# Attention values of four heads in one load: 64 value products of 256 columns over four column groups, one collecting product, and the output projection all 512 wide

## The chip, the cores and the metric

The kernel runs on one core of one Trainium2 chip. The metric is the device time of one execution in microseconds (us). The kernel before takes 235.41 us, the median of three runs (235.37 to 235.57). The profile shows one execution of the same program: its span, from the first instruction to the last, is 233.7 us. All times inside the program are counted from the start of that span.

## The reference

One decoding step of a transformer block for two batch rows (`B = 2`), everything in float32. A conditioning vector `c` gives six modulation vectors. The attention has 32 query heads that share 8 key and value heads (four query heads to one), and looks at the last 4096 positions of the cache. After it come the output projection `wo` and a two-layer network with SiLU.

```python
mod = (_silu(c) @ w_mod).reshape(2, 6, 1, -1)         # sa, ca, ga, sb, cb, gb
h = _layernorm(x) * (1 + ca) + sa
q = (h @ wq), split into 32 heads of 128
k = k_cache[:, :, Sk - W:, :]                         # W = 4096, 8 heads, each used by 4 query heads
v = v_cache[:, :, Sk - W:, :]
p = _softmax(q . k * 128 ** -0.5)
o = p . v                                             # 32 heads of 128
x = x + ga * (o @ wo)                                 # wo: 4096 x 512
h = _layernorm(x) * (1 + cb) + sb
x = x + gb * (_silu(h @ w1) @ w2)                     # w1: 512 x 1792, w2: 1792 x 512
```

What is read from HBM is almost all of the work: 32 MiB of keys, 32 MiB of values, 8 MiB of `wq`, 8 MiB of `wo`, 6 MiB of `w_mod`, and 3.5 MiB each of `w1` and `w2`.

## The kernel before

**The ring.** All large loads go through one buffer in SBUF, `slots`, of 8 slots with 4096 floats per partition each (L68). `stream(n)` (L70) hands out the next n slots; for an even n it first moves on to a multiple of n. All these loads are issued on one queue, that of SyncE (SP in the profile), in the order of the code. A load into a slot waits on SP until everything that read the slot's last content is done, and so does every load behind it.

**The stages.** First `w_mod` (3 slots) and `wq` (4 slots) are loaded, and the modulation and the queries are computed. Then come eight steps (`STEPS`, one for each pair of key heads and batch row), and behind them the output projection, the second normalization and the network.

**One step.** `load_pair` (L77) loads the keys of two heads, 4 MiB, 32768 bytes per partition, into two slots, and, one step later, the values of the same two heads in the same way. `keys(s, j)` (L356) transposes a quarter of the keys on VectorE (DVE), 32x32 blocks at a time; there are four buffers for these quarters (L55). `scores(s, j)` (L366) multiplies them on TensorE (PE). `maxima` (L382) and `exponentials` (L400) make the softmax's numerators, and `turn` (L415) brings them into the form in which they are the weights of the value products: `ptb`, 16 blocks of 32 columns, two buffers of it.

**The value products.** `weighted(s)` (L442) multiplies the values of one step: 16 products of 512 columns each. Every product writes 32 partitions of the result; four products that follow one another write four different groups of 32 partitions, which TensorE works on side by side (four column groups). Since the data are float32, the profile counts two matmul instructions for one product. ScalarE (ACT) copies the 128x512 result to SBUF, and `collect(s)` (L460) adds it with four small products into `o_all`, which is kept in PSUM over all eight steps.

**The order.** `inorder` keeps the instructions of one engine in the order of the code. The loop (L475 to L500) runs the scores of step s ahead of the value products of step s-1. The values of the last step are loaded last, and `weighted(7)` and `collect(7)` stand at the end.

**Behind the steps.** `on` (L534) divides `o_all` by the sums of the softmax, and four products with `quad` (`oq`, L537) and a copy turn it into `oTn`, the weights of the output projection. `busy(n)` (L562) issues n products that write to `junk` and are read by nobody; `busy(6)` (L576) stands ahead of the projection. The projection with `wo` (loaded in two pieces, 24 and 8 of its 32 rows per partition) has 28 products of 512 columns over four column groups (`acc_o`, L577) and 16 products of 128 columns that write straight to `ao` (L586). `gather` (L546) adds the four groups of `acc_o` into `ao`: ACT copies the first half to SBUF, DVE the second, and four products follow. Then come, each waiting for the one before, the transposition `aoT`, the mean `mean_b`, `hT_b`, the products with `w1` (`hid`, L627), the SiLU on DVE and ACT, whose result is `uT`, and the products with `w2`: `acc_yw` (8 of 14 rows of `w2`), `acc_y`, another `gather`, and `acc_l`. `w1` is loaded in two pieces and `w2` in four, of which the first (8 rows) is the largest. In the ring `wo` takes the slots 0 to 3, the first piece of `w1` the slots 4 and 5, its second the slot 6, the first piece of `w2` the slot 7, and the other pieces of `w2` the slots 0 to 2.

Of the kernel before, what the change touches and what calls it, by code (L numbers as in the profile page):

```python
# [8 lines left out]
F32 = mybir.dt.float32  # L9
# [14 lines left out]
def adaln_block(  # L24
# [30 lines left out]
    ktp = ctx.enter_context(tc.tile_pool(name="ktp", bufs=4))  # L55
# [47 lines left out]
    for b in range(B):  # L103
# [46 lines left out]
    id16, mix = const([P, 16], "id16"), const([P, 16, 2], "mix")  # L150
# [3 lines left out]
    nc.gpsimd.tensor_mul(  # L154
        mix,
        id16[:, :, None].to_broadcast([P, 16, 2]),
        half[:, None, :].to_broadcast([P, 16, 2]),
    )
    odd = const([P, 2], "odd")
    nc.vector.tensor_reduce(  # L160
        odd, ident.rearrange("p (a r) -> p r a", r=2), axis=AX.X, op=ALU.add
# [13 lines left out]
    selh = const([P, 4, 4 * HQ - 8], "selh")  # L175
    nc.gpsimd.memset(selh, 0.0)
    nc.gpsimd.tensor_copy(
        selh[:, :, 2 * HQ - 8 : 2 * HQ].rearrange("p m (e g) -> p m e g", e=2),
        id4.rearrange("p (e m g) -> p m e g", e=2, g=G),
# [26 lines left out]
    ptb = [const([P, 16, 2, 16], f"ptb{i}") for i in range(2)]  # L206
# [132 lines left out]
    o_all = bank("O", "o_all")[:, :DH]  # L339
# [26 lines left out]
    def scores(s, j):  # L366
# [3 lines left out]
        i, b = divmod(s, B)  # L370
        for c in range(2):
            for e in range(2):
                r, h = 64 * e + 32 * c, 2 * i + e
# [41 lines left out]
    def turn(s):  # L415
# [9 lines left out]
        tp = bank("C", f"pT{s}")[:, : 2 * P]  # L425
        for i in range(4):
            inorder(nc.tensor.matmul(  # L427
                tp[32 * i : 32 * i + 32, :],
                mix.rearrange("p v e -> p (v e)"),
                zp.rearrange("p y t x -> p (y t) x")[:, :, 4 * i : 4 * i + 4],  # L430
                start=True,
                stop=True,
            ))
        for e in range(2):
            inorder(nc.scalar.activation(  # L435
                ptb[s % 2][:, :, e, :],
                tp.rearrange("p (w z) -> p w z", z=16),
                AF.Copy,
                scale=odd[:, e : e + 1],
            ))  # L440
# [291 lines left out]
```

## Time and profile before

| what | us |
|---|---|
| median of three runs | 235.41 (235.37 to 235.57) |
| span of the profiled execution | 233.7 |
| DVE busy | 115.6 (49% of the span) |
| PE busy | 161.1 (69%), in 1070 matmul instructions |
| ACT busy | 28.5 (12%) |
| POOL busy | 10.5 (4%) |
| read from HBM | 97.53 MB, 417 GB/s over the span |
| share of DMA waits in the chain that ended last | 60% |

A row of a timeline gives the start in us from the span's start, the duration in us, the engine, the line of the program, the operation, the result and the operands, and how many instructions are merged in it; in brackets stands how long the engine was idle before, and what ended the wait. PE is matmul, PEld the loading of weights for it. A row of the windows gives a stretch, its length, the busy time of the engines in it with the count of instructions, the TensorE clock that was granted (1.00 is full speed), the mean busy share of the core's 16 DMA engines, and what they moved. Over a short stretch the share can come out a little above 1.

### The profile page before, as it was taken

To read this page: it belongs to the slowest core of one execution; us is meant where nothing else is said; L and a number is where in the kernel's file an instruction comes from. 1 tells how busy PE (TensorE), PEld (TensorE's weight loads), DVE (VectorE), ACT (ScalarE), POOL (GpSimd) and SP (SyncE) were. 2 spreads that over 40 slices of the span, in tenths; PEclk is the share of its full clock that TensorE was granted. 3 is DMA by queue.
4 is the path that set the end of the run, shared out by engine and by line. 5 is a ranking of instruction groups with operands and counts; after the bars stand their busy time and mean duration, and the time that the engine had idled before them with its cause. 6 is when DMAs were issued, how large, how long until landed. Compare 5 with 4: busy or idle time off the path is not lost.

```text
span 233.7 us, 2571 instructions
## 1 busy us (share of the span) xinstructions
PE 161.1 (69%) x1070; PEld 43.3 (19%) x1070; DVE 115.6 (49%) x179; ACT 28.5 (12%) x64; POOL 10.5 (4%) x35
## 2 busy tenths in 40 slices
PE   0004916859577839797598749759759779789684
PEld 0001401201111111211120201202112122324222
DVE  0007240278894758695197089259559540101232
ACT  2000210000311120120210201111020120102020
POOL 2004710000000000000000000000000000000000
PEclk9999985979999977999979999988997997999999
DMA  7998998999999999999999999999999999989991
GB/s 269 446 542 359 404 494 359 446 444 421 415 421 449 446 437 415 426 426 446 449 437 409 418 437 449 449 421 412 426 444 449 443 421 437 463 367 437 424 404 57
DMA packets 3794, 97.68 MB, mean 418 GB/s; under 512 B 432, under 2 KB 456, under 8 KB 968
## 3 DMA queue, kind: packets, MB, share of 16 engines
q1 hardware_dynamic: 3768, 97.53, 97.1%
q8 instruction: 8, 0.13, 0.2%
q14 instruction: 2, 0.02, 0.0%
q10 hardware_dynamic: 16, 0.00, 0.0%
HBM read 97.53 MB, written 0.00 MB: 417 GB/s over the span
## 4 chain that ended last, share of the span: by engine, by line
DMA 60%; issue 18%; DVE 14%; PE 6%; POOL 0%; SPq 0%; POOLq 0%; ACT 0%
DMA slots<-in_A_k_cache_dram 22%; DMA slots<-in_A_wq_dram 15%; DMA slots<-in_A_v_cache_dram 12%; DMA slots<-in_B_w_dram 12%; DVE kT L361 11%; PE o L448 2%; PE q L302 2%; DVE zp L420 1%; PE acc_yw L661 1%; DVE xp L418 1%; PE qr L323 0%; PE acc_y L671 0%; DVE qT L315 0%; POOL qg L319 0%; SPq L109 0%
## 5 line engine op out<-in xcount | busy, mean ns | idle before, releaser
L361 DVE STREAM_TRANSPOSE kT<-slots 128x1024 f32<-128x1024 f32 x64 | 73.7, 1212 | 23.7 <-DMA slots<-in_A_k_cache_dram 23.6
L374 PE MATMUL s<-kT,qbd 128*32 128x512 f32 x256 | 68.6, 693 | 19.1 <-DVE kT L361 18.0
L448 PE MATMUL o<-slots,ptb 128*32 128x512 f32 x256 | 30.8, 624 | 2.1 <-DMA slots<-in_A_v_cache_dram 2.1
L374 PEld LDWEIGHTS s<-kT,qbd 128*32 128x32 f32 x256 | 9.6, 113 | 68.4 <-DVE kT L361 63.4
L269 PE MATMUL m_a<-slots,scT 128*32 128x256 f32 x32 | 4.4, 506 | 20.5 <-DVE scT L261 20.5
L302 PE MATMUL q<-slots,hq_T 128*32 128x512 f32 x64 | 8.3, 680 | 7.0 <-DMA slots<-in_A_wq_dram 7.0
L448 PEld LDWEIGHTS o<-slots,ptb 128*32 128x32 f32 x256 | 8.1, 114 | 17.9 <-issue 17.8
L404 ACT COPY bias<-bp 128x1 f32<-128x1 f32 x8 | 1.3, 159 | 77.0 <-PE bp L402 77.0
L384 DVE TENSOR_REDUCE mx<-s 128x1 f32<-128x512 f32 x8 | 5.5, 691 | 9.6 <-PE s L374 9.6
L565 PE MATMUL junk<-quad,id 128*32 128x512 f32 x22 | 10.2, 595 | 0.0
L420 DVE TENSOR_TENSOR zp<-xp,quarter 128x1024 f32<-128x1024 f32 x8 | 9.8, 1225 | 0.2
L435 ACT ACTIVATE ptb<-pT,odd 128x256 f32<-128x256 f32 x16 | 6.7, 472 | 25.6 <-PE pT L427 25.6
L255 DVE STREAM_TRANSPOSE cT<-xc 128x128 f32<-128x128 f32 x1 | 0.4, 401 | 16.7 <-DMA xc<-in_c_dram 16.7
L427 PE MATMUL pT<-zp,mix 128*32 128x256 f32 x64 | 5.7, 428 | 3.6 <-DVE zp L420 3.5
L458 ACT COPY ob<-o 128x512 f32<-128x512 f32 x8 | 4.7, 585 | 26.1 <-PE o L448 26.1
L272 PE MATMUL m_sp<-slots,scT 128*32 128x512 f32 x32 | 7.4, 738 | 0.0
L386 PE MATMUL mT<-ident,mx 128*1 128x128 f32 x16 | 3.0, 270 | 6.3 <-DVE mx L384 6.3
L315 DVE STREAM_TRANSPOSE qT<-q 128x512 f32<-128x512 f32 x2 | 1.4, 717 | 11.7 <-PE q L302 10.2
L418 DVE STREAM_TRANSPOSE xp<-pr 128x512 f32<-128x512 f32 x8 | 5.5, 686 | 3.4 <-ACT pr L406 3.4
L579 PE MATMUL acc_o<-slots,oTn 128*32 128x512 f32 x56 | 6.2, 593 | 0.7 <-DMA slots<-in_A_wo_dram 0.7
L466 PE MATMUL o_all<-ob,selh 128*64 128x128 f32 x64 | 6.0, 316 | 0.8 <-ACT ob L458 0.8
L550 DVE COPY acc_o_sb<-acc_o 128x256 f32<-128x256 f32 x1 | 0.4, 425 | 12.4 <-ACT acc_o_sb L549 12.4
(140 smaller groups left out, 93.8 us busy)
## 6 DMA issues: line engine op xcount, KB each, us to landing
slots<-in_A_k_cache_dram SPq DMA_DIRECT2D x8, 4096.0 KB, 27.4
slots<-in_A_v_cache_dram SPq DMA_DIRECT2D x8, 4096.0 KB, 27.6
slots<-in_w_mod_dram SPq DMA_DIRECT2D x1, 6144.0 KB, 17.1
slots<-in_A_wo_dram SPq DMA_DIRECT2D x1, 6144.0 KB
slots<-in_B_w_dram SPq DMA_DIRECT2D x1, 2688.0 KB
slots<-in_A_wo_dram SPq DMA_DIRECT2D x1, 2048.0 KB, 29.5
slots<-in_B_w_dram SPq DMA_DIRECT2D x1, 2048.0 KB
slots<-in_B_w_dram SPq DMA_DIRECT2D x1, 896.0 KB
```

What stands on the lines that cost most here:

```text
L272: nc.tensor.matmul(m_sp[r, :], scT[:, k, :], cd[:, g], start=(k == 0), stop=(k == 3))
L302: nc.tensor.matmul(q_ps[n][32 * g : 32 * g + 32, :], hq_T[:, k, :], wv[:, n, g], start=(k == 0), stop=(k == 3),)
L361: inorder(nc.vector.transpose(kT[s, j][:, 32 * c : 32 * c + 32, :], kt[s].rearrange("p (n j r) -> p j n r", j=4, r=32)[:, j, 32 * c : 32 * ...
L374: inorder(nc.tensor.matmul(s_ps[s][r : r + 32, :], qbd[h // 4][:, h % 4, b, j, :], kT[s, j][:, 32 * c : 32 * c + 32, e:32:2], start=(j == ...
L418: inorder(nc.vector.transpose(xp, pr[s]))
L420: inorder(nc.vector.tensor_mul(zp, xp[:, None, :, 0:16].to_broadcast([P, 4, 16, 16]), quarter[:, :, None, None].to_broadcast([P, 4, 16, 16 ...
L427: inorder(nc.tensor.matmul(tp[32 * i : 32 * i + 32, :], mix.rearrange("p v e -> p (v e)"), zp.rearrange("p y t x -> p (y t) x")[:, :, 4 * ...
L435: inorder(nc.scalar.activation(ptb[s % 2][:, :, e, :], tp.rearrange("p (w z) -> p w z", z=16), AF.Copy, scale=odd[:, e : e + 1],))
L448: inorder(nc.tensor.matmul(o_ps[s][r : r + 32, :], ptb[s % 2][:, w].rearrange("p e z -> p (e z)"), vt[s].rearrange("p (c w m f d) -> p c f ...
L466: inorder(nc.tensor.matmul(o_all[r : r + 64, :], selh[:, m, lo : lo + 2 * HQ], o_sb[s][:, m * DH : (m + 1) * DH], start=(s == 0 and m < 2) ...
L565: inorder(nc.tensor.matmul(junk[0:32, :], id4, quad.rearrange("p m y -> p (m y)"), start=True, stop=True,))
L579: inorder(nc.tensor.matmul(acc[32 * g : 32 * g + 32, :], oTn[:, q, :], wot[q], start=(q < 4), stop=(q >= 24),))
```

## The change

**Loads.** `load_heads` takes the number of heads: keys still come two heads at a time (two slots, 32768 bytes per partition), values four heads at a time (four slots, 65536 bytes per partition, 8 MiB). The steps now run through all heads of one batch row before the other, so that two neighbouring steps share one load of values. Since `wq` ends at slot 7, the keys always fall on slots 0 to 3 and the values always on slots 4 to 7.

**Value products.** `turn` makes 64 blocks of weights for a pair of steps (`ptb`, one buffer, each step fills half of the columns), with eight products of 256 columns in place of four, and two ACT copies of twice the size. `weighted` runs once for two steps: 64 products of 256 columns over four column groups. ACT copies the result in two halves and scales each (`own`). `collect` is one product of 256 columns, and `o_all` has 64 rows of 256, whose two halves DVE adds (`of_all`) ahead of `on`.

**Behind the steps.** The projection has 32 products of 512 columns and no small ones. `gather` copies both halves on ACT, and for the projection issues one `busy` product ahead of its four products.

```diff
-    ktp = ctx.enter_context(tc.tile_pool(name="ktp", bufs=4))
+    ktp = ctx.enter_context(tc.tile_pool(name="ktp", bufs=3))
...
-    def load_pair(cache, s):
-        i, b = divmod(s, B)
-        t = stream(2)
+    def load_heads(cache, b, h, heads):
+        t = stream(heads)
         nc.sync.dma_start(
             t,
-            cache[b, 2 * i : 2 * i + 2, SK - W :, :].rearrange("e (u n) d -> u e (n d)", u=P // 2),
+            cache[b, h : h + heads, SK - W :, :].rearrange("e (u n) d -> u e (n d)", u=P // heads),
         )
         return t
...
+    id16, mix = const([P, 16], "id16"), const([P, 2, 8, 2, 2], "mix")
...
+    quad4 = const([P, 4], "quad4")
+    nc.vector.tensor_reduce(
+        quad4, ident.rearrange("p (a r) -> p r a", r=4), axis=AX.X, op=ALU.add
     )
...
+    selh = const([P, 2 * LO + 16], "selh")
...
+    own = const([P, 2], "own")
+    nc.vector.tensor_reduce(
+        own, id4.rearrange("p (e m g) -> p m e g", e=4, m=2), axis=AX.XY, op=ALU.add
     )
...
-    ptb = [const([P, 16, 2, 16], f"ptb{i}") for i in range(2)]
+    ptb = const([P, 32, 2, 4, 8], "ptb")
...
-    o_all = bank("O", "o_all")[:, :DH]
+    o_all = bank("O", "o_all")[: B * HQ, : 2 * DH]
...
-    def fetch(s):
+    def head(s):
+        b, i = divmod(s, HKV // 2)
+        return b, 2 * i
+    def fetch_keys(s):
         if s < STEPS:
-            kt[s] = load_pair(k_cache, s)
-        if s > 0:
-            vt[s - 1] = load_pair(v_cache, s - 1)
+            kt[s] = load_heads(k_cache, *head(s), 2)
+    def fetch_values(i):
```

The body of `turn` behind `zp`, `weighted` and `collect` after the change:

```python
    def turn(s):
...
        tp = bank("C", f"pT{s}")
        for f in range(2):
            for i in range(4):
                inorder(nc.tensor.matmul(
                    tp[32 * i : 32 * i + 32, 2 * P * f : 2 * P * (f + 1)],
                    mix[:, f].rearrange("p u a e -> p (u a e)"),
                    zp.rearrange("p y t x -> p (y t) x")[:, :, 4 * i : 4 * i + 4],
                    start=True,
                    stop=True,
                ))
        for e in range(2 * (s % 2), 2 * (s % 2) + 2):
            inorder(nc.scalar.activation(
                ptb[:, :, :, e, :].rearrange("p w y z -> p (w y) z"),
                tp.rearrange("p (v z) -> p v z", z=8),
                AF.Copy,
                scale=quad4[:, e : e + 1],
            ))
    def weighted(i):
        o_ps[i] = bank("D", f"o{i}")[:, : 2 * DH]
        runs = vt[i].rearrange(
            "p (h c w y m f d) -> p (h c) f w y m d", h=2, c=2, w=4, y=2, m=2, f=2
        )
        for v in range(64):
            w, r = v // 2, 32 * (v % 4)
            inorder(nc.tensor.matmul(
                o_ps[i][r : r + 32, :],
                ptb[:, w, v % 2].rearrange("p e z -> p (e z)"),
                runs[:, w // 8, w // 4 % 2, w % 4, v % 2],
                start=(v < 4),
                stop=(v >= 60),
            ))
        o_sb[i] = once.tile([P, 2 * DH], F32, tag="wide", name=f"ob{i}")
        for m in range(2):
            c = slice(m * DH, (m + 1) * DH)
            inorder(nc.scalar.activation(
                o_sb[i][:, c], o_ps[i][:, c], AF.Copy, scale=own[:, m : m + 1]
            ))
    def collect(i):
        b, h = head(2 * i)
        lo = LO - (HQ * b + G * h)
        inorder(nc.tensor.matmul(
            o_all, selh[:, lo : lo + 2 * HQ], o_sb[i], start=(i == 0), stop=(2 * i + 2 == STEPS)
        ))
```

The loop, and what stands behind it:

```diff
-    fetch(0)
...
+    fetch_keys(0)
+    fetch_keys(1)
+    fetch_values(0)
     keys(0, 0)
-    for s in range(STEPS + 1):
-        if s < STEPS:
-            fetch(s + 1)
-            scores(s, 0)
-        if s > 0 and s != STEPS - 1:
-            turn(s - 1)
-        if s > 1:
-            collect(s - 2)
-        if s == 2:
+    for s in range(STEPS):
+        scores(s, 0)
+        for j in range(1, 4):
+            keys(s, j)
+            scores(s, j)
+        fetch_keys(s + 2)
+        maxima(s)
+        exponentials(s)
+        if s % 2 == 0:
+            keys(s + 1, 0)
+        turn(s)
+        if s == 1:
             place(1)
-        if s < STEPS:
-            for j in range(1, 4):
-                keys(s, j)
-                scores(s, j)
-            maxima(s)
-            exponentials(s)
-        if s < STEPS - 2:
-            keys(s + 1, 0)
-        if s > 0:
-            weighted(s - 1)
-        if s == STEPS - 2:
-            turn(s)
-            keys(s + 1, 0)
-    collect(STEPS - 1)
+        if s % 2:
+            weighted(s // 2)
+            fetch_values(s // 2 + 1)
+            collect(s // 2)
+            if s + 1 < STEPS:
+                keys(s + 1, 0)
...
-    on = once.tile([P, B, DH], F32, tag="xp", name="on")
+    nc.tensor.matmul(
+        lp[:R, 0:1], rx.rearrange("p b i e g -> p (b i e g)"), ones, start=True, stop=True
+    )
...
+    of_all = once.tile([R, DH], F32, tag="zp", name="of_all")
+    nc.vector.tensor_reduce(
+        of_all, o_all.rearrange("r (m d) -> r d m", m=2), axis=AX.X, op=ALU.add
+    )
+    on = once.tile([R, B, DH], F32, tag="xp", name="on")
     for b in range(B):
-        nc.vector.tensor_scalar(on[:, b, :], o_all, rlb[:, b : b + 1], None, op0=ALU.mult)
+        nc.vector.tensor_scalar(on[:, b, :], of_all, rlb[:, b : b + 1], None, op0=ALU.mult)
...
-    def gather(acc, wide, name, start, stop):
...
+    def gather(acc, wide, name, start, stop, fill=0):

         sb_ = once.tile([P, D], F32, tag="wide", name=name)
-        nc.scalar.copy(sb_[:, : D // 2], wide[:, : D // 2])
-        inorder(nc.vector.tensor_copy(sb_[:, D // 2 :], wide[:, D // 2 :]))
+        for c in (slice(0, D // 2), slice(D // 2, D)):
+            inorder(nc.scalar.copy(sb_[:, c], wide[:, c]))
+        if fill:
+            busy(fill)
...
-    for q in range(28):
...
             start=(q < 4),
-            stop=(q >= 24),
+            stop=(q >= 28),
         ))
-    for q in range(28, 32):
-        for g in range(4):
-            inorder(nc.tensor.matmul(
-                ao[32 * g : 32 * g + 32, :],
-                oTn[:, q, :],
-                wot[q][:, g * P : (g + 1) * P],
-                start=(q == 28),
-                stop=False,
-            ))
-    gather(ao, acc, "acc_o_sb", False, True)
+    gather(ao, acc, "acc_o_sb", True, True, fill=1)
```

Two places show how the instructions move. The first is the queue of SP at the end of the loop: the last loads of keys and values and the first of the weights behind them. Before (the last column is partitions x floats per partition):

```order
L82 DMA slots<-in_A_k_cache_dram 128x1x8192
L82 DMA slots<-in_A_v_cache_dram 128x1x8192 x2
L93 DMA slots<-in_A_wo_dram 128x12288
L93 DMA slots<-in_A_wo_dram 128x4096
L93 DMA slots<-in_B_w_dram 128x5376
```

After:

```order
L81 DMA slots<-in_A_k_cache_dram 128x1x8192 x2
L81 DMA slots<-in_A_v_cache_dram 128x1x16384
L92 DMA slots<-in_A_wo_dram 128x12288
L92 DMA slots<-in_A_wo_dram 128x4096
L92 DMA slots<-in_B_w_dram 128x5376
```

Before, the last two loads ahead of `wo` are values of 4 MiB each; after, it is one load of values of 8 MiB, and both last loads of keys stand ahead of it.

The second place is PE from the last value products to the products with `w1` (`o` are the value products, `acc_o` and `ao` the projection, `hid` the products with `w1`). Before:

```order
L448 MATMUL o_900<-slots,ptb_150 32x512 x16
L466 MATMUL o_all<-ob_917,selh 64x128 x4
L539 MATMUL oq<-on,quad 128x64 x4
L565 MATMUL junk<-quad,id_58 32x512 x6
L579 MATMUL acc_o<-slots,oTn 32x512 x28
L588 MATMUL ao<-slots,oTn 32x128 x16
L552 MATMUL ao<-acc_o_sb,id_58 32x128 x4
L565 MATMUL junk<-quad,id_58 32x512
L614 MATMUL mean_b<-ks,mean_139 128x2
L565 MATMUL junk<-quad,id_58 32x512
L627 MATMUL hid<-slots,hT_b 32x448 x8
```

After:

```order
L464 MATMUL o_976<-slots,ptb 32x256 x64
L482 MATMUL o_all<-ob_1041,selh 64x256
L547 MATMUL oq<-on,quad 128x64 x4
L559 MATMUL junk<-quad,id_58 32x512 x6
L589 MATMUL acc_o<-slots,oTn 32x512 x32
L559 MATMUL junk<-quad,id_58 32x512
L576 MATMUL ao<-acc_o_sb,id_58 32x128 x4
L559 MATMUL junk<-quad,id_58 32x512
L615 MATMUL mean_b<-ks,mean_142 128x2
L559 MATMUL junk<-quad,id_58 32x512
L628 MATMUL hid<-slots,hT_b 32x448 x8
```

The 16 value products of 512 columns at the end have become 64 of 256; the 16 small products of the projection are gone and four wide ones have come; a product that writes `junk` stands between the projection and its gathering.

More of the change, by code (lines that the diff above doesn't have):

```diff
@@ L539, in adaln_block @@
         nc.tensor.matmul(
-            oq, quad[:, j, :], on[:, :, 32 * j : 32 * j + 32], start=(j == 0), stop=(j == 3)
+            oq, quad[:R, j, :], on[:, :, 32 * j : 32 * j + 32], start=(j == 0), stop=(j == 3)
         )
@@ L576, in adaln_block @@
     busy(6)
-    for q in range(28):
+    for q in range(32):
         g = q % 4
```

119 lines of the change are left out of this document (43 added, 76 removed).

## The prediction

> **What bounds the kernel now.** I read the page's slices and the windows first (is there a stretch in which the DMA engines are idle?), then the chain that ended last, then the timeline of the tail, where the change puts its longest new piece.
>
> ```profile
> span 233.7 us, 2571 instructions
> DMA  7998998999999999999999999999999999989991
> 58.00:192.00 134.00, 102.00 (x610) 23.86 (x606) 89.77 (x105) 19.91 (x50) 0.49 (x2) 0.94 1.01 435
> 126.84 27.70 DMA slots<-in_A_k_cache_dram
> 154.54 0.02 issue
> 165.61 27.61 DMA slots<-in_A_v_cache_dram
> 193.21 0.14 issue
> 193.35 5.37 PE o L448 x32
> 198.74 27.57 DMA slots<-in_B_w_dram
> 226.30 0.14 issue
> 226.44 1.92 PE acc_yw L661 x16
> ```
>
> The DMA engines are busy from the first slices to the last but one. In the eight steps (58 to 192 us) their share is 1.01 at 435 GB/s, with PE busy 102 and DVE 90 of 134 us. A load of keys lands at 154.54, the last values at 193.21: four loads of 4 MiB in 38.67 us, 9.67 us each. So the steps are bound by the transfers and compute is hidden. Only what stands behind a last landing counts: the chain leaves the DMA at 193.21 for the value products of the last step, goes back to it, and leaves it at 226.30 for good, when the large piece of `w2` lands. Whether compute or that landing ends last is read from the tail:
>
> ```profile
> 186.21 3.64 PE L448 MATMUL o<-slots,ptb 128*32 128x512 f32 x32
> 188.81 0.13 PEld L448 LDWEIGHTS o<-slots,ptb 128*32 128x32 f32 x4 [0.30 <-issue]
> 189.88 22.84 SPq L93 DMA_DIRECT2D slots<-in_B_w_dram  x6
> 193.35 5.34 PE L448 MATMUL o<-slots,ptb 128*32 128x512 f32 x32 [2.11 <-DMA slots<-in_A_v_cache_dram]
> 198.80 0.58 ACT L458 COPY ob<-o 128x512 f32<-128x512 f32 x1 [7.53 <-PE o L448]
> 199.44 0.66 PE L466 MATMUL o_all<-ob,selh 128*64 128x128 f32 x8 [0.75 <-ACT ob L458]
> 201.91 5.34 PE L565 MATMUL junk<-quad,id 128*32 128x512 f32 x12
> 207.91 6.22 PE L579 MATMUL acc_o<-slots,oTn 128*32 128x512 f32 x56 [0.66 <-DMA slots<-in_A_wo_dram]
> 213.91 1.08 PE L588 MATMUL ao<-slots,oTn 128*32 128x128 f32 x32
> 214.23 0.37 ACT L549 COPY acc_o_sb<-acc_o 128x256 f32<-128x256 f32 x1 [14.85 <-PE acc_o L579]
> 214.71 0.42 DVE L550 COPY acc_o_sb<-acc_o 128x256 f32<-128x256 f32 x1 [12.43 <-ACT acc_o_sb L549]
> 215.65 0.32 DVE L604 STREAM_TRANSPOSE aoT<-ao 128x128 f32<-128x128 f32 x1 [0.52 <-PE ao L552]
> 217.11 1.04 PE L565 MATMUL junk<-quad,id 128*32 128x512 f32 x2
> 217.42 0.17 DVE L618 TENSOR_TENSOR hT_b<-dT,cbT 128x8 f32<-128x8 f32 x1
> 219.46 1.71 PE L627 MATMUL hid<-slots,hT_b 128*32 128x448 f32 x16 [1.30 <-DMA slots<-in_B_w_dram]
> 225.36 0.21 DVE L657 TENSOR_TENSOR uT<-z,sgh 128x28 f32<-128x28 f32 x1
> 226.44 1.92 PE L661 MATMUL acc_yw<-slots,uT 128*32 128x512 f32 x16 [0.76 <-DMA slots<-in_B_w_dram]
> ```
>
> The reader is to see three covers, each a place where PE waited for a transfer although the compute ahead of it was done. The `junk` products stream 12 times 0.43 us (the pace in the PEld row: 0.30 idle and 0.13 loading for each group) from 201.91, so PE was free at 207.07 and waited for `wo` until 207.91: cover 0.84. `hT_b` was ready at 217.59 and the two `junk` passes were through at 217.97, but `hid` waited for `w1` until 219.46: cover 1.49. `uT` was ready at 225.57, some 0.1 later PE could have begun, and `acc_yw` began at 226.44: cover 0.77. In all 3.1 us. A delay of the last value products costs nothing up to that, and its full length beyond.
>
> **The change, part by part.** I add up against the profiled execution; the 1.7 us between its span (233.7) and the median (235.41) lie outside the program and are left as they are.
>
> *Loads.* Bytes are the same, and 435 GB/s over 134 us leave no pauses to remove: 0, so the last values land at 193.21 again. Values now have one buffer of four slots, so `weighted` must be over before the next values can be issued; behind each load of values two of keys are queued, 2 x 9.67 = 19.3 us of transfer, against some 7 to 9 us of products. The first piece of `w1` (issued at 189.88 in the row above) now waits for the last value products, until about 202; ahead of it 8 MiB of `wo`, 19.3 us, run until about 212. That wait holds up all loads behind it on SP, but 10 us of transfers hide it: 0.
>
> *Steps.* Larger copies for `ptb`, eight `pT` products for four, one fewer `kT` buffer: hidden by the transfers, since the busiest engine (PE, 102 of 134 us) has 32 us to spare there: 0.
>
> *Last value products.* They now process 8 MiB, not 4, behind the last landing. What is the price of 64 products of 256 columns, 128 instructions, in groups of four?
>
> ```profile
> 27.56 0.39 PE L269 MATMUL m_a<-slots,scT 128*32 128x256 f32 x3
> 27.78 0.39 PE L269 MATMUL m_a<-slots,scT 128*32 128x256 f32 x3
> 193.30:196.70 3.40, 3.35 (x19) 0.53 1.07 463
> 196.70:198.70 2.00, 1.99 (x20) 0.95 0.91 393
> ```
>
> The `m_a` products are also 256 columns over four column groups; at full clock one group follows the other after 0.22 us, half of the 0.43 of 512 columns. So 32 groups need 6.9 us and 0.2 for the last to end, 7.08 against 3.64 (the row at 186.21, full clock): +3.44. At 193.3 PE had been idle, and ran 3.4 us at clock 0.53, which cost 5.34 - 3.64 = 1.70. PE is idle there again, so the same 1.70 stays in the sum: 8.78 for 5.34. Bounds: no slow stretch at all, -1.7; one of twice the length, +1.7.
>
> *From there to `oTn`.* ACT copies two halves of 128 columns for 0.58 in one piece; `collect` streams 2 x 256 columns, as each half of the array did before (4 x 128): 0 each. New is the sum of the halves on DVE:
>
> ```profile
> L384 DVE TENSOR_REDUCE mx<-s 128x1 f32<-128x512 f32 x8 | 5.5, 691 | 9.6 <-PE s L374 9.6
> L116 DVE TENSOR_REDUCE id<-ident 128x32 f32<-128x128 f32 x1 | 0.4, 368 | 0.0
> ```
>
> 256 elements lie between 368 and 691 ns, about 475; less something for `on`, which then reads half the rows: +0.4 (0.2 to 0.6).
>
> *Projection.* The six `junk` products stay ahead of it in PE's order. The shift so far is 3.84, less the cover of 0.84: it begins 3.0 later, at 210.9, and `wo` has landed by then or lands on the way. Four wide products for sixteen narrow: eight instructions more in two groups, +0.86. The narrow ones (213.91 to 214.99) covered the two copies of `gather`; now the copies stand bare behind the last product, 0.1 less than before since both are ACT's, and the new `junk` product runs beside them. So `aoT` starts at 215.65 + 3.0 + 0.86 - 0.1 = 219.4.
>
> *To the end.* +3.73 there, less the cover of 1.49 at `hid`: +2.24; less 0.77 at `acc_yw`: +1.47. In the last `gather` the second copy is about 0.08 shorter: -0.08. **Sum: +1.4**, a span of 235.1 and a time of **236.8 us** (+0.6%).
>
> **A rule against the change.** The Trainium skill, TensorE: Matmul & The Clock Gate, Part 3 (The mechanism), says that weights load beside a running matmul only when the row group differs; all these products use all rows, so by it four loads would stand bare ahead of each group. The trace disagrees: the PEld row shows 0.13 within a pace of 0.43, which is the streaming alone.
>
> **The rivals.**
>
> *Weight loads are not hidden at 256 columns.* There are 32 groups with loads of 0.13 in a pace of 0.215 that leaves little room. If they stand bare, 32 x 0.13 = +4.2 more, all beyond the covers: 241.0. Against it stand the `m_a` rows. Chance 0.06.
>
> *The values' single buffer opens gaps.* If products, their weights and `place(1)` together outlast the 19.3 us of keys, each of the three later loads of values starts late; at 2 us each, 242.8. The 10 us of room speak against it. Chance 0.04.
>
> *The 65536-byte load lands earlier: not slower.* The load of `wq` has such rows too:
>
> ```profile
> 1.93 35.23 DMA slots<-in_A_wq_dram
> 48.23 2.37 DVE L361 STREAM_TRANSPOSE kT<-slots 128x1024 f32<-128x1024 f32 x2 [1.25 <-DMA slots<-in_A_k_cache_dram]
> ```
>
> It lands at 37.16, and the keys behind it only 11.07 us later, though a load takes 9.67: as if `wq` were 1.4 ahead of the stream. If the last values come 1.4 earlier for that reason, the delay of 1.47 is gone and `acc_yw` waits for `w2` again: 235.4, or 235.3 with the shorter copy. It decides from 1.0 us on. Against it: it is one event, and may be a hold-up of the keys. Chance 0.18 (0.14 of it within 0.2%).
>
> *Fewer loads save a fixed price: faster.* If each load cost 2 us beyond its bytes, four fewer save 8: 227.4. The 435 GB/s leave no room for it. Chance 0.02. The Trainium skill, DMA: Bandwidth & Descriptors, Anatomy of one DMA, fits 2.0 us plus the bytes at 436 GB/s to one DMA; back to back the trace shows 4.19 MB in 9.67 us, the bytes alone.
>
> Something else, around no change: 0.04.
>
> **How the numbers follow.** The forecast holds 0.66, with 235.9 to 238.5 as its own range (the slow stretch shorter or longer by half, the reduction's bounds). The range reaches down to the rival that is not slower: 235.2 to 238.5. What a measurement of this kernel can tell is about 0.2%, 0.47 us. Slower: 0.66 + 0.06 + 0.04 = 0.76. Within: 0.14 and 0.03 of the rest, 0.17. Faster: 0.04 + 0.02 + 0.01 = 0.07.
>
> **What would show it.** The last `o` group should start near 193.3 and take 8.8 us with a first stretch near clock 0.5; `acc_o` should start near 210.9 with no wait for `wo`; `hid` near 221.7 with no wait for `w1`; `acc_yw` should wait for `uT`, near 227.9, not for a DMA. The DMA row should stay at 9 through the steps. An `o` group over 11 us speaks for the weight loads, digits under 9 for the single buffer, a landing near 192 for the earlier load. Any of them makes the prediction wrong.

## The result, and the profile after

The changed kernel takes 241.56 us (median of six runs, 240.73 to 245.92), against 235.44 us (235.30 to 235.66) for the kernel before on the same chip: a ratio of 1.0247, with an interval from 1.0231 to 1.0263. One of the six (245.92 us) is a slow run (over 1.5% above the fastest), as is one run each of x2, x3, x4 and x9 below, the profiled ones of x3 and x9 among them; the ratios use the fast runs alone, and the median of the five fast ones here is 241.41, 6.0 us more than before. The prediction said slower, but by 1.4, and its range ended at 238.5.

The page of the profiled execution (240.73 us) first: the span, the share of the DMA engines in 40 slices, and the shares of the chain that ended last.

```profile
span 238.9 us, 3043 instructions
...
DMA  7998989999998999999999998999999999999930
...
PE 60%; DVE 15%; DMA 15%; ACT 6%; issue 2%; SPq 0%; DVEq 0%; ACTq 0%
```

The transfers still run through the steps as before: the DMA row has its 9 in all slices but a few. Yet the chain, which was 60% DMA, is now 60% PE. Something on the engines ends after the transfers. The timeline from the landing of the keys of step 6 to the last value products, in the changed kernel, shows it:

```profile
164.44 9.13 DVE L373 STREAM_TRANSPOSE kT<-slots 128x1024 f32<-128x1024 f32 x8 [9.52 <-DMA slots<-in_A_k_cache_dram]
174.76 0.69 DVE L396 TENSOR_REDUCE mx<-s 128x1 f32<-128x512 f32 x1 [1.19 <-PE s L386]
...
176.28 2.35 DVE L373 STREAM_TRANSPOSE kT<-slots 128x1024 f32<-128x1024 f32 x2
178.57 0.66 DVE L430 STREAM_TRANSPOSE xp<-pr 128x512 f32<-128x512 f32 x1
179.26 1.23 DVE L432 TENSOR_TENSOR zp<-xp,quarter 128x1024 f32<-128x1024 f32 x1
180.40 6.87 DVE L373 STREAM_TRANSPOSE kT<-slots 128x1024 f32<-128x1024 f32 x6
...
188.47 0.69 DVE L396 TENSOR_REDUCE mx<-s 128x1 f32<-128x512 f32 x1 [1.20 <-PE s L386]
...
191.59 0.71 DVE L430 STREAM_TRANSPOSE xp<-pr 128x512 f32<-128x512 f32 x1 [1.53 <-ACT pr L418]
192.34 1.23 DVE L432 TENSOR_TENSOR zp<-xp,quarter 128x1024 f32<-128x1024 f32 x1
...
193.71 1.94 PE L440 MATMUL pT<-zp,mix 128*32 128x256 f32 x16 [0.94 <-DVE rl L535]
195.70 1.26 ACT L448 ACTIVATE ptb<-pT,quad 128x512 f32<-128x512 f32 x2 [4.14 <-PE pT L440]
197.02 8.45 PE L464 MATMUL o<-slots,ptb 128*32 128x256 f32 x128 [1.38 <-ACT ptb L448]
```

The bracket of the last row decides it: the products wait for ACT's copy into `ptb`, their weights, and not for a DMA as before. They start at 197.02 instead of 193.35, 3.67 later. From the landing of step 6's keys (DVE starts at 164.44, when its wait for the DMA ends) to the weights' end at 196.96 there are 32.5 us of work in sequence: 16 transpositions, two maxima, two exponentials, two turns. Behind that landing only the keys of step 7 and the last values are still to come, three loads' worth, 3 x 9.67 = 29.0 us. So the last values were there at about 193.4 (164.4 + 29.0); the weights came 3.5 us after them.

In the kernel before, the same piece of its timeline was:

```profile
173.93 9.13 DVE L361 STREAM_TRANSPOSE kT<-slots 128x1024 f32<-128x1024 f32 x8 [2.12 <-DMA slots<-in_A_k_cache_dram]
...
189.66 0.61 PE L427 MATMUL pT<-zp,mix 128*32 128x256 f32 x8
190.42 0.84 ACT L435 ACTIVATE ptb<-pT,odd 128x256 f32<-128x256 f32 x2
```

There the last products needed the weights of step 7 alone. From 173.93 to 191.26 these took 17.3 us, against 19.3 us of transfers behind the landing: 2 us to spare. The change joins two steps in each product. Two steps take nearly twice as long on the engines, but only three loads, not four, stand behind the landing that starts them.

The tail of the changed kernel:

```profile
206.91 0.42 DVE L539 TENSOR_REDUCE of_all<-o_all 64x128 f32<-64x256 f32 x1 [13.02 <-PE o_all L482]
208.98 4.91 PE L559 MATMUL junk<-quad,id 128*32 128x512 f32 x11
213.76 7.43 PE L589 MATMUL acc_o<-slots,oTn 128*32 128x512 f32 x61
222.49 0.32 DVE L605 STREAM_TRANSPOSE aoT<-ao 128x128 f32<-128x128 f32 x1 [13.13 <-PE ao L576]
224.50 2.01 PE L628 MATMUL hid<-slots,hT_b 128*32 128x448 f32 x16
230.95 1.92 PE L662 MATMUL acc_yw<-slots,uT 128*32 128x512 f32 x16
235.37 0.63 SPq L705 DMA_DIRECT2D out_dram<-yo  x1
```

In the kernel before, three places in this tail waited for a DMA: the covers of the prediction. None of these waits is left. The table sets each place against the kernel before (the output's DMA was issued at 231.07 there); its last column is the first experiment below.

| place | predicted shift | shift of the change | without step 7's turn (x1) |
|---|---|---|---|
| start of the last `o` | 0 | +3.67 | +0.26 |
| first `junk` | +3.84 | +7.07 | +4.25 |
| `aoT` | +3.73 | +6.84 | +4.01 |
| `hid` | +2.24 | +5.04 | +2.20 |
| `acc_yw` | +1.47 | +4.51 | +1.68 |
| output's DMA issued | +1.4 | +4.30 | +1.47 |
| end of the span | +1.4 | +5.2 | +1.7 |

### The profile page after: what moved, and what is told of

Read it like the earlier page. It is cut to its first block, busy times and chain, and to the rows that moved or that the text cites. A ratio compares the mean times of both kernels' runs of the same rounds, so it can differ in the third digit from the quotient of the medians.

```text
span 238.9 us, 3043 instructions
## 1 busy us (share of the span) xinstructions
PE 154.7 (65%) x1310; PEld 54.7 (23%) x1310; DVE 114.7 (48%) x180; ACT 30.5 (13%) x66; POOL 10.3 (4%) x35
## 4 chain that ended last, share of the span: by engine, by line
PE 60%; DVE 15%; DMA 15%; ACT 6%; issue 2%; SPq 0%; DVEq 0%; ACTq 0%
PE s L386 20%; PE o L464 15%; DMA slots<-in_A_wq_dram 15%; PE pT L440 7%; DVE zp L432 4%; PE q L309 4%; PE junk L559 4%; DVE kT L373 3%; PE acc_o L589 3%; DVE mx L396 2%; DVE xp L430 2%; ACT ptb L448 2%; ACT pr L418 2%; PE hid L628 1%; PE mT L398 1%
## 5 line engine op out<-in xcount | busy, mean ns | idle before, releaser
L386 PE MATMUL s<-kT,qbd 128*32 128x512 f32 x256 | 48.9, 718 | 2.7 <-DVE kT L373 2.4
L464 PE MATMUL o<-slots,ptb 128*32 128x256 f32 x512 | 36.2, 452 | 4.1 <-ACT ptb L448 4.1
L440 PE MATMUL pT<-zp,mix 128*32 128x256 f32 x128 | 15.5, 631 | 26.4 <-DVE zp L432 25.4
L464 PEld LDWEIGHTS o<-slots,ptb 128*32 128x32 f32 x512 | 17.9, 130 | 23.3 <-issue 8.5
L386 PEld LDWEIGHTS s<-kT,qbd 128*32 128x32 f32 x256 | 11.0, 127 | 36.9 <-DVE kT L373 22.8
L448 ACT ACTIVATE ptb<-pT,quad 128x512 f32<-128x512 f32 x16 | 10.1, 683 | 35.2 <-PE pT L440 35.2
L309 PE MATMUL q<-slots,hq_T 128*32 128x512 f32 x64 | 9.7, 776 | 7.3 <-DMA slots<-in_A_wq_dram 7.3
L440 PEld LDWEIGHTS pT<-zp,mix 128*32 128x32 f32 x128 | 5.4, 158 | 30.0 <-issue 30.0
L589 PE MATMUL acc_o<-slots,oTn 128*32 128x512 f32 x64 | 7.9, 594 | 0.0
L474 ACT ACTIVATE ob<-o,own 128x128 f32<-128x128 f32 x8 | 2.5, 364 | 35.4 <-PE o L464 35.4
```

What stands on the lines that cost most here:

```text
L309: nc.tensor.matmul(q_ps[n][32 * g : 32 * g + 32, :], hq_T[:, k, :], wv[:, n, g], start=(k == 0), stop=(k == 3),)
L386: inorder(nc.tensor.matmul(s_ps[s][r : r + 32, :], qbd[h // 4][:, h % 4, b, j, :], kT[s, j][:, 32 * c : 32 * c + 32, e:32:2], start=(j == ...
L440: inorder(nc.tensor.matmul(tp[32 * i : 32 * i + 32, 2 * P * f : 2 * P * (f + 1)], mix[:, f].rearrange("p u a e -> p (u a e)"), zp.rearrang ...
L448: inorder(nc.scalar.activation(ptb[:, :, :, e, :].rearrange("p w y z -> p (w y) z"), tp.rearrange("p (v z) -> p v z", z=8), AF.Copy, scale ...
L464: inorder(nc.tensor.matmul(o_ps[i][r : r + 32, :], ptb[:, w, v % 2].rearrange("p e z -> p (e z)"), runs[:, w // 8, w // 4 % 2, w % 4, v % ...
L589: inorder(nc.tensor.matmul(acc[32 * g : 32 * g + 32, :], oTn[:, q, :], wot[q], start=(q < 4), stop=(q >= 28),))
```

## The experiments

The theory, A: the last products are late because their weights need both steps' chains. The rivals are named in the expectations. Where not said otherwise, a kernel is an edit of the changed one, and each ratio is to the kernel before on the same chip.

**x1: step 7's turn left out.** Its half of the weights stays that of step 5.

```diff
-        turn(s)
+        if s < STEPS - 1:
+            turn(s)
```

> The changed kernel without the weights of the last step (turn of step 7 is left out, so the last value products use old weights in half of their columns). Theory A (the last value products start 3.5 us late because the two steps ahead of them take 32.6 us from the landing of their first keys, while the transfers in between take only 29.1 us): the products start at the landing, near 193.4 us instead of 197.0, and the time falls by 3 to 3.6 us, to about 238. Theory B (the start is not what costs; all of the extra time lies behind it, in 8 MiB of products and the projection): start and time within 1 us of the changed kernel, about 241.

Measured: 237.26 us (236.67 to 237.78), ratio 1.0077 [1.0058, 1.0096]. In its timeline the last products start at the landing again:

```profile
193.61 9.11 PE L464 MATMUL o<-slots,ptb 128*32 128x256 f32 x128 [1.09 <-DMA slots<-in_A_v_cache_dram]
...
228.12 1.92 PE L663 MATMUL acc_yw<-slots,uT 128*32 128x512 f32 x16
...
232.54 0.63 SPq L706 DMA_DIRECT2D out_dram<-yo  x1
```

With the weights' wait gone, 4.1 us of the 6.0 are gone (0.7 of them lie behind the output's issue; see x9 and x10). What is left, 1.85 us over the kernel before, is close to the 1.4 that I had for the whole change, and the table's last column follows my own terms place by place. The work of the turn itself is left out too, but all of it stands ahead of the start of the products.

**x2: the value products of the first three pairs left out.** Only the last pair's stay.

```diff
-            weighted(s // 2)
+            if s == STEPS - 1:
+                weighted(s // 2)
             fetch_values(s // 2 + 1)
-            collect(s // 2)
+            if s == STEPS - 1:
+                collect(s // 2)
```

> The changed kernel with the value products of the first three pairs of steps left out (only the last pair's products and their collection remain). Theory A (each pair starts anew when its first keys land, so late products of one pair do not push the next): the last products still start near 197 us and the time stays within 1 us, 240 to 242. Theory C (a backlog: PE runs through all pairs without a pause, as the chain that ended last reads, and 9 us of products in each pair push everything behind them): the start moves to the landing at 193.4 or to where the keys allow it, and the time falls by 3 us or more, to 238 or less.

Measured: 241.94 us (241.16 to 245.43), ratio 1.0265 [1.0247, 1.0283]: no gain.

```profile
197.04 9.46 PE L464 MATMUL o<-slots,ptb 128*32 128x256 f32 x128 [1.38 <-ACT ptb L448]
```

The start is the same to 0.02 us without 384 earlier instructions of PE, so no delay adds up from pair to pair. The chain of the changed kernel's page runs through the products of all four pairs and gives PE 60%, and would make one believe that it does. Each pair begins anew at the landing of its keys.

**x3: no six `junk` products ahead of the projection.**

```diff
-    busy(6)
```

> The changed kernel without the six products nobody reads that stand ahead of the projection. Before the change they ended 0.84 us before wo landed; after it they stand between oTn (ready at 209.4) and the projection (214.2), though wo has landed. Theory A: the projection starts near 209.5, 4.7 us earlier, and the time falls by about 4.5 us to 237. Rival D (without them the TensorE clock falls and the projection and what follows run at half speed): the projection takes 10 us or more instead of 7.4 and the time falls by 2 us or less.

Measured: 238.23 us (237.55 to 241.28), ratio 1.0109 [1.0092, 1.0126]; 3.3 less than the change, not the 4.5 of theory A, and more than the 2 of rival D.

```profile
210.02 1.78 PE L547 MATMUL oq<-on,quad 64*128 64x64 f32 x8 [1.11 <-DVE on L544]
...
212.16 9.46 PE L588 MATMUL acc_o<-slots,oTn 128*32 128x512 f32 x64 [0.36 <-DVE oTn L550]
```

The projection now begins as soon as `oTn` is there. In the changed kernel `oTn` is ready at 209.36 and the bulk of the projection begins at 213.76, so some 4.4 us stood to be won, and 3.3 were. Where the other 1.1 us went is not shown. The 9.46 us of the projection here, for about 7.9 in the changed kernel, cannot be put down to the missing products: in this execution the four `oq` products ahead of them are slow already (1.78 us for 1.07).

**x4: values in two halves.** Each half has its own load of 32768 bytes per partition and its own 32 products, in the order of loads of the kernel before; the second half's products run in the next pair's first step, the last pair's at the end.

```diff
+        if s % 2 == 0 and s > 0:
+            weighted(i - 1, 1)
+            fetch_values(i, 1)
...
         if s % 2:
-            weighted(s // 2)
-            fetch_values(s // 2 + 1)
-            collect(s // 2)
+            weighted(i, 0)
+            fetch_values(i + 1, 0)
```

> The changed products and projection, but each load of values in two halves of 32768 bytes per partition, the queue in the old order (keys and half values by turns) and the 64 products in two parts of 32, of which the second runs inside the softmax of the next step; only the last 32 stand behind the last landing. Theory A (late start and 8 MiB behind the last landing are the whole loss): the last 32 products start at the landing near 193.3, take 5.3 us, the three covers swallow what the wide projection and the sum of the halves add, and the time is 235 to 236. Theory E (the 256-column products, the wide projection or the gathering cost by themselves): 237 or more.

Measured: 240.02 us (239.34 to 243.86), ratio 1.0195 [1.0174, 1.0215]. A miss: theory A had 235 to 236, and the time lies in the range of E.

```profile
174.50 2.37 DVE L385 STREAM_TRANSPOSE kT<-slots 128x1024 f32<-128x1024 f32 x2 [6.13 <-DMA slots<-in_A_k_cache_dram]
...
195.20 8.83 PE L477 MATMUL o<-slots,ptb 128*32 128x256 f32 x128 [1.38 <-ACT ptb L460]
```

Yet the rows show the wait of theory A: all 64 products still ran together and still waited for `ptb`. A half of the values has 32 of the 64 blocks of weights, but each block has columns of both steps. So the first half cannot go ahead either: step 7's own chain, with step 6's turn in the middle of it, takes 20.7 us from its keys' landing (174.50 to 195.20), and the two halves behind it 19.3.

**x5: halves, and the keys of both steps ahead of the previous pair's second half.** The copies into `ptb` are taken out of `turn` into `weights`, since `ptb` must keep the previous pair's weights until its second half is through.

```diff
         if s % 2 == 0:
             keys(s + 1, 0)
-        turn(s)
...
+            turn(s)
+        else:
+            if i > 0:
+                weighted(i - 1, 1)
+            fetch_values(i, 1)
+            weights(s - 1)
+            turn(s)
+            weights(s)
...
+            weighted(i, 0)
+            fetch_values(i + 1, 0)
```

> The values in halves of 32768 bytes per partition as in x4, but now the keys of both steps of a pair are queued ahead of the second half of the values before (so k6, k7, second half of v2, first half of v3, second half of v3), and step 7's chain runs while 29 us of transfers stand between its keys' landing and the end. Theory A (the last products wait for weights that need both steps' chains): k7 lands near 164.4, all weights are ready near 187, the first 32 products run near 187, and the last 32 start at the landing, near 193.4, and take 4 to 5.3 us; 235.2 to 236.0 in all, since the first half's work is hidden and the transfers' floor is that of the kernel before. Rival E (the order of the queue does not matter; 64 products of 256 columns with weights of four heads cost the time wherever they stand): 239 to 242, as x4. Rival F (the waits for slots that the new order makes open pauses in the stream): last landing after 195, 237 to 239.

Measured: 242.0 us (240.96 to 243.72), ratio 1.0281 [1.0248, 1.0313]. From its timeline (the row of SPq is the issue of the last load of values):

```profile
182.05 3.66 PE L481 MATMUL o<-slots,ptb 128*32 128x256 f32 x64
185.77 0.54 SPq L89 DMA_DIRECT2D slots<-in_A_v_cache_dram  x1
...
190.07 3.66 PE L481 MATMUL o<-slots,ptb 128*32 128x256 f32 x64 [0.81 <-ACT ptb L464]
199.51 5.34 PE L481 MATMUL o<-slots,ptb 128*32 128x256 f32 x64 [5.78 <-DMA slots<-in_A_v_cache_dram]
```

The weights are now in time: the first half's products run at 190.07 and the second half's wait 5.78 us for a DMA, not for `ptb`. But what rival F describes came true, if not its time (237 to 239). The load they wait for goes into the half buffer that the products at 182.05 read. It could be issued only at 185.77, when the load ahead of it was already through, and the stream paused: the page's slice from 180.3 to 186.3 us shows 155 GB/s, its neighbours 431 and 349. The lateness moved from the weights into the transfers. The time lies in the range of E (239 to 242), but the landing alone accounts for it: the last products start 6.16 later than in the kernel before, and the output's DMA is issued 5.97 later (237.04).

**x6: five `junk` products ahead of step 7's turn.**

```diff
         exponentials(s)
+        if s == STEPS - 1:
+            for _ in range(5):
+                inorder(nc.tensor.matmul(
+                    o_bank[64:96, :],
+                    id4,
+                    quad.rearrange("p m y -> p (m y)"),
+                    start=True,
+                    stop=True,
+                ))
```

> After with five products that nobody reads ahead of step 7's turn, while PE waits for step 7's exponentials; they write rows of the bank that nothing else uses. Nothing is left out. Theory A with the clock as a term of its own: the eight pT products of step 7 run at a higher clock (1.94 down to 1.0 to 1.3 us) and the 64 value products without their slow first stretch (8.45 down to 7.1), so the span falls by 1.5 to 2.3 and the time to 239.2 to 240.0. Rival (the clock is not kept by such products, or what they win is lost again by a lower clock in the projection): 241 to 241.7.

Measured: 240.35 us (239.82 to 242.01), ratio 1.0211 [1.0186, 1.0235]. By the ratios (1.0247 for the change) that is about 0.85 us less, and the span is 238.1 for 238.9; 1.5 to 2.3 were expected.

```profile
190.44 4.48 PE L501 MATMUL o_all<-quad,id 128*32 128x512 f32 x10
...
195.06 1.07 PE L441 MATMUL pT<-zp,mix 128*32 128x256 f32 x16
197.51 7.11 PE L465 MATMUL o<-slots,ptb 128*32 128x256 f32 x128 [1.39 <-ACT ptb L449]
```

Both sizes came as expected: `pT` 1.07 for 1.94, the products 7.11 for 8.45, without a slow stretch. But the five products lasted until 194.9 and held `pT` back from 193.71 to 195.06, 1.35 us, so the products ended only 0.85 earlier (204.62 for 205.47). By this pace three of them would have fitted the gap; whether three keep the clock up was not run.

**x7: the kernel before with the wide projection alone.** The 16 narrow products go, `gather` copies both halves on ACT.

```diff
-    for q in range(28):
+    for q in range(32):
...
-    gather(ao, acc, "acc_o_sb", False, True)
+    gather(ao, acc, "acc_o_sb", True, True, fill=1)
```

> The kernel before with one part of the change alone: all 32 products of the output projection 512 wide, and gather with both copies on ACT and one more product that nobody reads. My prediction put +0.86 on the two groups more and -0.1 on the copies, which the wait of hid for w1 (1.49) swallows whole: 235.2 to 235.6. Rival (the added time is not swallowed, because w1's wait was shorter than the row says or the chain to aoT is longer than 0.76): 236.0 to 236.5.

Measured: 235.88 us (235.71 to 236.17), ratio 1.0014 [1.0006, 1.0023].

```profile
208.30 7.07 PE L581 MATMUL acc_o<-slots,oTn 128*32 128x512 f32 x64 [0.72 <-DMA slots<-in_A_wo_dram]
...
219.47 1.71 PE L620 MATMUL hid<-slots,hT_b 128*32 128x448 f32 x16 [0.32 <-DMA slots<-in_B_w_dram]
...
226.53 1.92 PE L654 MATMUL acc_yw<-slots,uT 128*32 128x512 f32 x16 [0.84 <-DMA slots<-in_B_w_dram]
```

The wider projection is swallowed: `hid` starts at 219.47 as it did at 219.46, and still waits for `w1`. The median is 0.26 us above that of the kernel before on the same chip (235.62), and outside the expected 235.2 to 235.6; the span, 233.7, is that of the kernel before, so the profile shows no place for it.

**x8: x5 with the previous pair's second half between the scores.** Eight products at a time, the last eight behind the maxima, and the next half is fetched right behind them.

```diff
             scores(s, j)
+            if s % 2 and i > 0:
+                weighted(i - 1, 1, j - 1)
```

> As x5, but the 32 products of the second half of a pair's values stand between the scores of the next pair's second step, eight at a time, and not behind its bias. In x5 the last load could be issued only at 186.4, when these products were over, and landed at 199.5. Theory A (only a weights' chain or a late issue puts the last products behind the transfers): the products of pair 2 end near 181, the last load is issued there, 4 us ahead of the end of the load before it, and lands at 193.4 to 194.5; the last 32 products start there and take 3.6 to 5.3; 235.3 to 237.0 in all, no slower than before by more than 0.7%. Rival E (64 products of 256 columns cost their time wherever they stand): 239 or more. Rival G (the eight-product pieces hold up the scores and so the weights of pair 3 by 3 us or more): the first half's products run at 193 or later and the last 32 behind them, 237 to 239.

Measured: 239.22 us (238.54 to 239.39), ratio 1.0146 [1.0125, 1.0167].

```profile
181.33 1.03 PE L481 MATMUL o<-slots,ptb 128*32 128x256 f32 x13
...
196.21 5.35 PE L481 MATMUL o<-slots,ptb 128*32 128x256 f32 x64 [3.10 <-DMA slots<-in_A_v_cache_dram]
```

The buffer is free 3.3 us earlier than in x5 (182.4 for 185.7), and the last load lands 3.3 us earlier. That ties the landing to the buffer, but it still comes at 196.2, 2.9 later than in the kernel before, and the expected 235.3 to 237.0 was missed. Rival G is out: the first half's products ran at 189.00. The time lies in the range of E (239 or more), but the rows speak against E: nothing but the DMA holds the second half, and the output's DMA is issued 2.56 later than in the kernel before (233.63), no more than the landing is late. No version that I ran beats the kernel before.

**x9 and x10: what ends the span.** Beyond the shift of 4.30 at the output's DMA, the change loses another 0.9 us: the span ends 3.5 us after that issue, 2.6 in the kernel before. In the profiles up to here this went with the number of DVE instructions. x9 is the changed kernel with one of them given to GpSimd, x10 the kernel before with one done twice.

```diff
-    nc.vector.tensor_add(x1, x_sp, ax)
+    nc.gpsimd.tensor_add(x1, x_sp, ax)
```

> After with one instruction moved: the sum x1 in the tail is GpSimd's and no longer DVE's, so that DVE has 179 instructions as in the kernel before and not 180. Nothing is left out, and the sum is needed only 10 us later. Theory H (in the profiles so far the span ends 3.4 to 3.7 us after the output's DMA is issued wherever DVE has 180 instructions, and 2.6 to 2.9 us after it where it has 177 to 179, since a load of instructions falls beside the output's packets): 2.6 to 2.9 us here, and 240.4 to 241.0 in all, 0.6 to 0.9 less than after. Rival (the 0.9 us go with the lateness of the products or with the queue, not with the count): 3.4 to 3.7 us, and 241.2 to 241.8.

> The kernel before with one more DVE instruction, the reduction group done twice, near 20.6 us, where DVE waits anyway: 180 instead of 179. Theory H: the span ends 3.4 to 3.7 us after the output's DMA is issued, 236.1 to 236.6 in all. Rival: 2.6 to 2.9 us, 235.3 to 235.7.

Measured: x9 241.51 us (241.02 to 245.97), ratio 1.0262 [1.0246, 1.0279]; x10 235.95 us (235.72 to 236.45), ratio 1.0022 [1.0011, 1.0033]. The time of x9 lies in the range of its rival, that of x10 in neither range. The output's row of x10, whose span is 234.0, and that of x9, whose span is 244.2:

```profile
231.16 0.64 SPq L707 DMA_DIRECT2D out_dram<-yo  x1
```

```profile
240.60 0.63 SPq L705 DMA_DIRECT2D out_dram<-yo  x1
```

With 180 instructions (x10) the end comes 2.8 us after the issue, with 179 (x9) 3.6 us after it: the count does not decide it, and theory H as it stands falls. What it named as the reason does go with the late end. In the DMA view of the stretch from the output's issue to the end of the span, the changed kernel and x9 both show one packet of the queue q14, of the kind `instruction`, beside the output's own 12:

```profile
q14 instruction: 1, 0.01, 0.9%
q1 hardware_dynamic: 12, 0.00, 0.5%
```

x10 shows the output's packets alone:

```profile
q1 hardware_dynamic: 12, 0.00, 0.6%
```

The same holds in all twelve profiles: the eight that have such a packet in this stretch end 3.3 to 3.7 us after the issue, and the four that have none (the kernel before, x1, x7 and x10) end 2.5 to 2.9 us after it. No experiment moved that packet alone, so the cause is not shown.

## Why the prediction was wrong

**The step that failed** is "Steps": "hidden by the transfers, since the busiest engine (PE, 102 of 134 us) has 32 us to spare there: 0". A busy sum of a stretch says whether the work fits into the stretch. It does not say when the last of it ends. The last products need the end of a chain that starts at a landing, and that chain grew from one step to two. It put the start 3.67 us late (x1 shows it by taking the wait away, x2 that nothing else had piled up). The rows were there in the profile before: 17.3 us from the keys' landing to the weights of step 7, out of 19.3. I priced the copies and the `pT` products as busy time, and never asked which weights a joined product waits for. So "the last values land at 193.21 again" was right within 0.3 (in x1 the products start at their landing, at 193.61 for 193.35), and "The last `o` group should start near 193.3" was wrong.

**A second loss was not in the sum**: the 0.9 us between the output's issue and the end. By the profile the shift at the end, 5.2, exceeds the forecast's 1.4 by 3.8: 2.9 at the output's issue, and 0.9 behind it. The 2.9 are less than the 3.67 because my other terms, less what the covers took, came to 0.8 less than I had; the sizes follow below. The median of 241.41 exceeds the forecast by 4.6; the further 0.8 is mostly that the profiled execution (240.73) is the fastest of the six, and no trace shows where the others lost it.

**Loads: 0** was right. The stream does not starve: the last load of values is issued at 167.44, 6.7 us before the keys queued ahead of it are in (164.44 + 9.67), where I had estimated 10 us of room. The wait of `w1`'s first piece on SP costs nothing, since `hid` no longer waits for it. The rival "single buffer opens gaps" did not come true for the change itself. It did in x5 and x8, where the half buffers come free too late.

**Last value products: +3.44** was measured as +3.11 (8.45 for 5.34). At full clock 64 products take 7.11 (x6), where the working gave 7.08. The slow stretch that was kept in the sum is there, but it costs 1.34 (8.45 - 7.11) and not 1.70; part of it has passed with the `pT` products (1.94 us at clock 0.50), and in x1, where the products come without them, they take 9.11. The rival on bare weight loads is out: in x6 the 128 loads take 4.03 us of PEld inside the 7.11 us of the products.

**From there to `oTn`: +0.4** was +0.29 (`o` ends to `junk`: 3.51 for 3.22); `of_all` took 0.42, estimated 0.475.

**Projection: +0.76** was 0.61 in the change (from `junk` to `aoT` -0.23, with the cover of 0.84 used up) and 0.60 in x7 (`acc_o` to `aoT`, 8.34 for 7.74). That a cover hides it as long as nothing else is late is shown by x7.

**The covers** came out right in sum partly by luck. That at `hid` was 1.80 (from `aoT` to `hid` 2.01 us for 3.81) and not 1.49, since `hid` did not wait for the two `junk` passes: it starts at 224.50, with the passes of 223.96 running until 225.00. That at `acc_yw` was 0.53 (from `hid` to `acc_yw` 6.45 us for 6.98) and not 0.77; `hid` itself took 2.01 for 1.71. Together they are 2.33, where I had 2.26. That a delay costs its full length beyond them was right: my own terms had used the covers up, and from x1 to the change `junk` comes 2.82 later and the output's DMA 2.83. That these are less than the 3.41 between the two starts comes from the products, which take 8.45 in the change and 9.11 in x1.

**Two slips in the working** did no harm. The +3.73 at `aoT` should read +3.76 by its own terms. The upper end of the range, 238.5, is the slow stretch of twice the length (+1.7), and not one longer by half (+0.85).

**The rival "lands earlier"** had no part: in x1, where PE waits for them, the values are there at 193.61. Nor did four fewer loads save a fixed price. The fit of 2.0 us per DMA that the prediction quotes from the Trainium skill, DMA: Bandwidth & Descriptors, Anatomy of one DMA, is stated there for DMAs on GpSimd's path. The loads here are issued by SyncE, and no run here shows a fixed price of theirs.

## What to carry to other kernels

When a change joins work of several steps into one instruction, follow the chain from the last landing that this instruction needs, and set its length against the transfers that are queued behind that landing; an engine's idle share says nothing about it. Moving loads so that such a chain gets more room also moves the moment at which each buffer must be free, and the lateness can come back as a pause in the stream. A `junk` product that is free while its engine waits for a transfer can cost time as soon as compute sets the end: leaving out six of them saved 3.3 us here.

## What the runs showed of the hardware that was not expected

The granted clock went with what PE had done in the few us before. In the windows of the changed kernel, and below them of x6 and of x1, the columns are the stretch, its length, PE's busy time with the count, the granted clock, the DMA share and GB/s.

```profile
193.71:197.02 3.31, 1.93 (x16) 0.50 1.06 460
197.02:205.50 8.48, 8.45 (x128) 0.84 0.89 384
```

```profile
193.71:197.02 3.31, 2.42 (x21) 1.00 0.96 416
197.51:204.62 7.11, 7.11 (x128) 1.00 1.02 438
```

```profile
193.61:197.00 3.39, 3.39 (x33) 0.50 1.04 449
197.00:202.72 5.72, 5.72 (x100) 0.94 0.97 415
```

Five products that nobody reads, issued from 190.44 on, are the only edit between the first two. The Trainium skill, TensorE: Matmul & The Clock Gate, Part 1 (The HAM clock gate), states that PE is held at half clock after an idle window of about 3.4 us and released after about as long a time of sustained work. The rows of x1 agree with the second half: 3.39 us of unbroken products at half clock. The first half they show only roughly, since PE was not quite idle: in the changed kernel it was busy for 0.25 of the 3.16 us ahead of 193.71.

The end of the span is the other surprise: 2.5 to 2.9 us after the output's issue in four of the kernels and 3.3 to 3.7 in the others, with nothing in the kernels' code behind the issue that differs. It goes with a packet of the kind `instruction` beside the output's packets, in twelve profiles of twelve.
